# Hash attention: the 32-column products of two pairs of heads gathered in one block of every odd pair

## The chip, the cores and the metric

The kernel runs on one core of a Trainium2 chip. The metric is the device time of one execution in microseconds (us), the median of several runs. A core has five engines with an instruction queue each: TensorE (PE in the profile; its weight loads are shown apart as PEld), VectorE (DVE), ScalarE (ACT), GpSimd (POOL) and SyncE (SP). Each works through its queue in order and waits on semaphores for the others. PE writes PSUM, which DVE and ACT read. DMA queues move data between the core's SBUF and the chip's memory; in this kernel SP issues most of them, POOL and ACT some.

## The reference

Attention with a hash mask, and then a layer with squared relu, all in float32:

```
B, H, S, D = 4, 8, 768, 64           # 6 hash bits, d_model 512, d_ff 2048
q_bits, k_bits = (q @ proj > 0), (k @ proj > 0)
mask   = bucket(q_bits)[:, :, :, None] == bucket(k_bits)[:, :, None, :]
scores = where(mask, q @ k^T / sqrt(D), -1e9)
attn   = softmax(scores);  x = attn @ v        # heads side by side: (3072, 512)
h = x @ w_in;  r = max(h, 0);  out = (r * r) @ w_out
```

A query attends only to keys whose six hash bits are all the same as its own.

## The kernel before, in words

The 32 heads are worked in 16 pairs (`pr` 0 to 15); a pair's two heads lie in the two halves of the 128 partitions. A loop over the pairs is the first stage; the second stage, the squared-relu layer in two levels of Strassen's method, follows and is not touched by the change, except that its tile of three x sums (`t_x`) has its memory allocated early.

The order of the instructions on every engine is written out by hand, inside a manual schedule. Each pair has six key tiles (`kt`), and each key tile two score products (`score`: four matmuls of the hash bits, four of the features, L438), each followed by one exponential on ACT (`weight`, L444) that writes half of a slot of a ring of four key tiles (`e`). Between the score products lie `attend` calls (L492): products of v with the weights, four small matmuls each, two per key tile. A score takes its PSUM buffer from a pool of two (`turn`); so a score waits for the exponential of the score before the last one. The hash products take a buffer of the same pool.

The pairs overlap. While pair `pr` begins, `attend` of key tiles 4 and 5 of pair `pr-1` (`old`) is still going on. After `attend(old, 5, 1)` the old pair is finished in this order: `keep_x` copies its result out of PSUM (ACT, L523); PE runs a block of products that use 32 of the array's columns instead of 64: `sum_up(old, 0)` (half of the softmax totals, L541), `hash_bits(pr + 1)` (the next pair's hash products, L368), `sum_up(old, 1)`; `signs` turns the hash products into signs (ACT, L387); `invert` transposes the totals and takes the reciprocal (DVE, L554, L558, L562); `spread` copies the reciprocals to the other rows (ACT, four small copies, L572); `normalize` transposes them back and scales x (DVE, L578, L584), and SP stores x to memory (`x_all`).

DVE also has, for every pair: `features` (transposes the loaded q and k, L352), `add_up` for key tiles 1 to 5 (adds the weights up to the totals, L475 and L480; a slot of the ring is free for new exponentials only when it has been added and attended to), and the preparation of the weights w_in and w_out, which arrive as 64-bit floats: `part_power` (L150), `part_top` (L176, L180), `round_weight` (L194, L197), and `sum_in` (L600, L617), 16 calls in all, dealt out to the pairs from 4 on. ACT works on the same weights: four `place_power` steps a pair (L166, L168), the last of which comes before `part_top`'s second instruction (L180), which rewrites the same tile. ACT's `weigh` (L393) scales the signs and POOL then places them as bits with eight small DMAs (`place_bits`, L404), for the next pair.

The queue of SP holds, in the order of the program, the loads of q and k (`load_pair`, eight DMAs of 128-byte pieces), of v (`load_values`), of the weights (`load_weight`), and the stores.

What the change touches: the pools and tiles `feat`, `total`, `x_raw`, `signed` and `t_x`; `features` (L349), `weigh` (L391), `sum_up` (L529), `invert` (L551), `normalize` (L574), the sharing out of `sums` (L630) and the body of the pair loop (from L685 on).

Of the kernel before, what the change touches and what calls it, by code (L numbers as in the profile page):

```python
# [8 lines left out]
FP32 = mybir.dt.float32  # L9
# [25 lines left out]
def kernel(  # L35
# [51 lines left out]
    w_out_49 = p_d.tile([7, P, 7, NQ, P], FP32, name="w_out_49")  # L87

    first = ExitStack()
    p_x = first.enter_context(tc.tile_pool(name="p_x", bufs=2))  # L90
# [17 lines left out]
    def spare(name):  # L108

        return ps_t.tile([P, 2, 512], FP32, name=name, tag="spare")  # L110
# [137 lines left out]
    signed = const.tile([P, 2, HS], BF16, name="signed")  # L248
    all_bits = [const.tile([P, 2, S], BF16, name=f"bits{i}") for i in range(2)]

    def constants():
# [20 lines left out]
            nc.vector.memset(e[:, :, :, HS:HS + 1], TINY)  # L272


    nat, feat, bits = {}, {}, {}

    def load_first():

        both = p_qk.tile([P, 2, 2, SB, D], FP32, name="qk_nat")
        for w, src in enumerate((q, k)):  # L280
            for h, queue in enumerate((nc.sync, nc.scalar)):
                queue.dma_start(
                    out=both[:, w, h].rearrange("p t d -> p (t d)"),
                    in_=src[0, h].rearrange("(p t) d -> p (t d)", t=SB),
                )
        nat[0, "qk"] = both
        feat[0] = p_f.tile([P, 2, S], FP32, name="feat")
# [96 lines left out]
    def signs(pr):  # L384


        nc.scalar.activation(  # L387
            out=signed, in_=hashed[pr, 0][:, :, 0:HS], func=ACTF.Sign, scale=HUGE, bias=lifts
        )

    def weigh():  # L391

        nc.scalar.activation(out=signed, in_=signed, func=ACTF.Copy, scale=gains)  # L393

    PARTS = (1, 0), (0, 0), (0, 1), (1, 1)

    def place_bits(pr, parts=PARTS):

        t = all_bits[pr % 2]
        for w, c in parts:  # L400
            bits[pr, w] = t[:, w]
            at = (2 * w + c) * NR_B
            for h in range(2):
                nc.gpsimd.dma_start(  # L404
                    out=t[h * D:h * D + NBITS + 1, w, c * HS:(c + 1) * HS],
                    in_=signed[at:at + NBITS + 1, h],
                )

    def first_keys(c, banks):
# [60 lines left out]
    def add_up(pr, kt):  # L470

        e = key_of(pr, kt)[:, :, :, 0:HS]
        if kt == 1:
            totals[pr] = p_n.tile([P, 2, 2, HS], FP32, name="total")
            nc.vector.scalar_tensor_tensor(  # L475
                out=totals[pr], in0=key_of(pr, 0)[:, :, :, 0:HS], scalar=SB * TINY,
                in1=e, op0=ALU.add, op1=ALU.add,
            )
        else:
            nc.vector.tensor_tensor(out=totals[pr], in0=totals[pr], in1=e, op=ALU.add)  # L480
# [38 lines left out]

    def keep_x(pr):  # L520

        raws_x[pr] = p_n.tile([P, 2, HS + 1], FP32, name="x_raw")
        nc.scalar.copy(out=raws_x[pr], in_=outs.pop(pr)[:, :, 0:HS + 1])  # L523

    NB = HS // 32
    QS = HS // 2
    onces = {}

    def sum_up(pr, s, whole=False):  # L529


        if s == 0:
            spares[pr] = spare("tot")
        halves = [(slice(0, P), s)] if whole else [
            (slice(r * HK, (r + 1) * HK), (r + s) % 2) for r in range(2)
        ]
        for rows, c2 in halves:
            for c in range(2):
                for h in range(2):
                    g = 2 * h + c  # L540
                    done = nc.tensor.matmul(  # L541
                        out=spares[pr][g * 32:(g + 1) * 32, c2, 0:QS], lhsT=ones[rows],
                        rhs=totals[pr][rows, h, c, c2 * QS:(c2 + 1) * QS],
                        start=whole or s == 0, stop=whole or s == 1, skip_group_check=True,
                    )
                    if s and (pr, "tot") in lasts:
                        part(lasts.pop((pr, "tot")), done)
        if not whole and s == 0:
            lasts[pr, "tot"] = done

    def invert(pr):  # L551

        flip = p_n.tile([P, HS], FP32, name="flip")
        nc.vector.transpose(  # L554
            out=flip.rearrange("p (c f) -> p c f", c=2), in_=spares.pop(pr)[:, :, 0:QS]
        )
# [17 lines left out]
    def normalize(pr):  # L574
# [7 lines left out]
        x_t = p_x.tile([P, S], FP32, name="x_t")  # L582
        raw = raws_x.pop(pr)
        nc.vector.scalar_tensor_tensor(  # L584
            out=x_t.rearrange("p (c f) -> p c f", c=2), in0=raw[:, :, 0:HS],
            scalar=raw[:, 0, HS:HS + 1], in1=over.rearrange("p (c f) -> p c f", c=2),
            op0=ALU.add, op1=ALU.mult,
        )
        nc.sync.dma_start(out=x_all[:, j, b * S:(b + 1) * S], in_=x_t)

    PLACE = 0, 5, 6, 1, 2, 3, 4

# [40 lines left out]
    xs = {}  # L633

    def load_x(i, fs=slice(0, NFT)):

        if i not in xs:
            x = p_c.tile([P, NFT, NCH], FP32, name="x")
            xs[i] = x, [p_c.tile([P, 2, NCH // 2], FP32, name=f"t_x{n}") for n in range(3)]
        nc.gpsimd.dma_start(out=xs[i][0][:, fs], in_=x_all[:, fs, i * NCH:(i + 1) * NCH])  # L640

    w_unit = {}
# [21 lines left out]
    with tc.manual_schedule():  # L664
# [18 lines left out]


        for pr in range(NP):  # L685
            more, old = pr + 1 < NP, pr - 1

            def beside(kt, s):
                if pr > 0:
                    attend(old, kt, s)  # L690

            if pr + 2 < NP:
                load_pair(pr + 2)
            if more and pr > 0:
                features(pr + 1)
            if pr == 0:
                first_score()
                first_keys(1, spare("hash"))
            else:
# [38 lines left out]
            if more:  # L738
                score(pr, 2, 0)
            if pr > 0:  # L740
                spread(old)
                attend(pr, 0, 0)
            else:
                attend(pr, 1, 0)
            score(pr, 2, 1)
            if pr > 0:
                attend(pr, 1, 0)
                if more:
                    weigh()
                else:  # L750
                    place_power(pr, 0, 0)
            else:
                hash_bits(1, turn("hash"))
                signs(1)
                weigh()
            score(pr, 3, 0)
            if pr > 0:
                place_power(pr, 0, int(not more))
# [44 lines left out]
        attend(pr, 2, 0)  # L803
        attend_whole(pr, SB - 2)
        add_up(pr, SB - 1)
        for s in range(2):
            sum_up(pr, s, True)
        invert(pr)
        for n in (1, 2, 3):
            sum_x(0, n)  # L810
# [876 lines left out]
```

## Time and profile before

| what | value |
|---|---|
| median of 3 runs | 856.3 us (855.09, 856.30, 856.32) |
| profiled execution, its own time | 855.04 us |
| its span in the trace | 853.2 us |
| busy in the span: PE, DVE, ACT, POOL | 847.0, 749.3, 402.4, 167.4 us |
| granted TensorE clock | 1.00 |
| period of a pair in the middle of the first stage | 19.03 us |
| DVE busy in the pair from 108.43 us on (one sum) | 18.41 us of 19.03 |
| first stage ends, second stage's first matmul | 315.43 us |

The profile lists busy time by engine, groups of instructions by source line, and the chain of work that ended last. The trace can also be asked for the instructions of an engine in order of time, merged where neighbours are alike: start, duration, engine, line, operation, output and inputs, number, and in brackets the idle time before it and what ended it. Busy time counts overlapping instructions once; DVE and ACT instructions that follow each other without a wait overlap by some 0.1 us, so that the distance from start to start is what one of them costs.

### The profile page before, as it was taken

The numbers are of one execution on the slowest core, as the hardware profiler recorded it, in microseconds if no ns is written. First come the engines' busy times: TensorE is split into PE (matmuls) and PEld (weight loads), VectorE is DVE, ScalarE is ACT, GpSimd is POOL, SyncE is SP. The second block draws the span as 40 slices with busy tenths as digits, with TensorE's granted clock in tenths as the row PEclk, the third lists the DMA queues.
The fourth block names the chain that finished last, engine by engine and source line by source line (L and its number), as shares of the span: only waits on it lengthen the run. The fifth ranks groups of instructions, "written<-read, shape, count | busy, mean of one in ns | idle before, by whom it ended". The sixth has DMA issues, their size and how long they took to land.

```text
span 853.2 us, 17058 instructions
## 1 busy us (share of the span) xinstructions
PE 847.0 (99%) x6625; PEld 526.5 (62%) x6625; DVE 749.3 (88%) x1025; ACT 402.4 (47%) x752; POOL 167.4 (20%) x282
## 2 busy tenths in 40 slices
PE   8999999999999999999999999999999999999998
PEld 4544444444444444444788866667888765668886
DVE  5999999999999988988899968888988788889777
ACT  6877777888877752222211145554111355541111
POOL 2311111123221101543122121111000311200003
PEclk9999999999999999999999999999999999999999
DMA  9776988979998526999976985437647865335467
GB/s 213 137 152 143 183 181 203 209 158 258 242 227 217 170 69 225 342 313 297 340 250 220 275 214 189 160 111 283 192 155 189 205 219 171 128 118 161 140 172 147
DMA packets 232052, 170.12 MB, mean 199 GB/s; under 512 B 164712, under 2 KB 189104, under 8 KB 231968
## 3 DMA queue, kind: packets, MB, share of 16 engines
q1 hardware_dynamic: 192272, 87.78, 41.3%
q0 software_dynamic: 16512, 42.45, 15.9%
q10 hardware_dynamic: 23184, 38.78, 14.6%
q8 instruction: 53, 0.87, 0.4%
q14 instruction: 31, 0.25, 0.1%
HBM read 127.14 MB, written 41.16 MB: 197 GB/s over the span
## 4 chain that ended last, share of the span: by engine, by line
PE 97%; DVE 1%; DMA 1%; issue 0%; ACT 0%; SPq 0%; ACTq 0%; DVEq 0%
PE acc L844 39%; PE st L438 18%; PE xo L492 15%; PE acc L1108 13%; PE acc L1061 9%; PE tot L541 2%; PE hash L368 1%; DMA out_dram<-h 1%; DMA qk_nat<-in_q_dram 0%; PE tp L324 0%; DVE h L1224 0%; DVE o L1210 0%; DVE tmp L1210 0%; DVE bits L418 0%; DVE sum L1210 0%
## 5 line engine op out<-in xcount | busy, mean ns | idle before, releaser
L444 ACT ACTIVATE e<-st 128x768 f32<-128x768 f32 x192 | 155.4, 810 | 57.8 <-PE st L438 54.7
L438 PE MATMUL st<-feat 64*64 64x384 f32 x1536 | 156.9, 483 | 0.1
L492 PE MATMUL xo<-e,v_nat 64*64 64x385 f32 (+1 forms) x1520 | 156.7, 483 | 0.0
L844 PE MATMUL acc<-b,leaf 128*128 128x256 f32 x600 | 133.0, 379 | 0.0
L844 PEld LDWEIGHTS acc<-b,leaf 128*128 128x128 f32 x600 | 113.9, 190 | 16.0 <-issue 0.5
L480 DVE TENSOR_TENSOR total<-total,e 128x1536 f32<-128x1536 f32 x64 | 111.8, 1746 | 4.3 <-ACT e L444 2.8
L404 POOL DMA_DIRECT2D bits<-signed x120 | 61.9, 520 | 216.8 <-ACT signed L393 199.9
L492 PEld LDWEIGHTS xo<-e,v_nat 64*64 64x64 f32 (+1 forms) x1520 | 55.5, 133 | 68.2 <-issue 60.2
L1108 PE MATMUL acc<-t_x,w_unit 128*128 128x512 f32 x192 | 90.9, 595 | 0.0
L438 PEld LDWEIGHTS st<-feat 64*64 64x64 f32 x1536 | 55.4, 133 | 38.9 <-issue 34.9
L844 PE MATMUL acc<-t,leaf 128*128 128x256 f32 x336 | 76.0, 379 | 0.0
L844 PEld LDWEIGHTS acc<-t,leaf 128*128 128x128 f32 x336 | 63.8, 190 | 8.8 <-issue 0.2
L921 DVE SCALAR_TENSOR_TENSOR b<-h 128x512 f32<-128x512 f32 x96 | 65.7, 691 | 3.0
L438 PE MATMUL st<-bits 64*64 64x384 bf16 x768 | 64.7, 325 | 0.3 <-DVE bits L422 0.2
L844 PE MATMUL acc<-x,w_unit 128*128 128x512 f32 x128 | 56.5, 593 | 0.0
L851 ACT COPY two<-acc 128x256 f32<-128x256 f32 (+1 forms) x29 | 12.5, 431 | 87.5 <-PE acc L844 65.9
L844 PE MATMUL acc<-b_t,leaf 128*128 128x256 f32 x240 | 53.8, 379 | 0.0
L1108 PEld LDWEIGHTS acc<-t_x,w_unit 128*128 128x128 f32 x192 | 35.8, 190 | 26.7 <-issue 23.0
L1229 POOL DMA_DIRECT2D out_dram<-h x24 | 15.5, 655 | 181.9 <-DVE h L1224 181.9
L844 PEld LDWEIGHTS acc<-b_t,leaf 128*128 128x128 f32 x240 | 45.6, 190 | 6.2
L851 ACT COPY one<-acc 128x256 f32<-128x256 f32 (+1 forms) x29 | 12.5, 431 | 78.2 <-PE acc L844 58.8
L438 PEld LDWEIGHTS <-bits 64*64 64x64 bf16 x768 | 23.2, 107 | 38.0 <-issue 37.9
(180 smaller groups left out, 1289.0 us busy)
## 6 DMA issues: line engine op xcount, KB each, us to landing
leaf<-w_out ACTq DMA_DIRECT2D x142, 256.0 KB, 3.1
raw<-in_moe_w_in_dram SPq DMA_DIRECT2D x8, 1024.0 KB, 6.7
raw<-in_moe_w_out_dram SPq DMA_DIRECT2D x8, 1024.0 KB, 7.9
w_unit<-w_in SPq DMA_DIRECT2D x16, 512.0 KB, 4.1
w_unit<-w_in SPq DMA_DIRECT2D x8, 896.0 KB, 9.0
w_out<-sums POOLq DMA_DIRECT2D x16, 448.0 KB, 8.0
v_nat<-in_v_dram SPq DMA_DIRECT2D x16, 384.0 KB, 5.2
x_all<-x_t SPq DMA_DIRECT2D x16, 384.0 KB, 3.3
```

What stands on the lines that cost most here:

```text
L404: nc.gpsimd.dma_start(out=t[h * D:h * D + NBITS + 1, w, c * HS:(c + 1) * HS], in_=signed[at:at + NBITS + 1, h],)
L438: nc.tensor.matmul(out=st[k * HK:(k + 1) * HK, h, 0:HS], lhsT=src[1][rows, key], rhs=src[0][rows, cut], start=first, stop=not first, skip_ ...
L444: nc.scalar.activation(out=key_of(pr, kt)[:, :, i, 0:HS], in_=st[:, :, 0:HS], func=ACTF.Exp, scale=scale)
L480: nc.vector.tensor_tensor(out=totals[pr], in0=totals[pr], in1=e, op=ALU.add)
L492: return nc.tensor.matmul(out=outs[pr][h * D:(h + 1) * D, c, 0:HS + 1], lhsT=nat[pr, "v_nat"][rows, h, kt * D:(kt + 1) * D], rhs=key_of(pr ...
L541: done = nc.tensor.matmul(out=spares[pr][g * 32:(g + 1) * 32, c2, 0:QS], lhsT=ones[rows], rhs=totals[pr][rows, h, c, c2 * QS:(c2 + 1) * QS ...
L844: nc.tensor.matmul(out=acc[to], lhsT=a(i), rhs=b(i), start=first and i == 0, stop=last and i == n - 1, skip_group_check=True,)
L851: nc.scalar.copy(out=t, in_=acc[of])
L921: nc.vector.scalar_tensor_tensor(out=out, in0=h, scalar=0.0, in1=h, op0=ALU.max, op1=ALU.mult)
L1061: nc.tensor.matmul(out=out, lhsT=w(a), rhs=b, start=start, stop=stop, skip_group_check=True)
L1108: nc.tensor.matmul(out=to, lhsT=w[:, PLACE[a], f], rhs=bt[b](f), start=first and f == 0, stop=last and f == NFT // 2 - 1, skip_group_check ...
L1229: queue.dma_start(out=out[at, m0 + a * 32:m0 + (a + 1) * 32].rearrange("(c i) j -> i c j", i=32), in_=ot[a * 32:(a + 1) * 32].rearrange("i ...
```

## The change

In every odd pair, PE runs one block with the totals of the two pairs before (`pr - 2` and `pr - 1`) and the hash products of the two pairs after (`pr + 1` and `pr + 2`); even pairs have no such block. The last pair has the totals of two pairs in the block and no hash products, and its own totals at the end as before.

For this, three feature buffers are used in turn instead of two, and two tiles of totals instead of one; the third feature buffer and the second totals tile lie in the memory of the three x sums of the second stage, which is now one tile and allocated at the start. `signed` and `x_raw` get a second buffer; x is scaled in place in `x_raw`, and the separate tile `x_t` is gone. `features` and `load_pair` run one pair further ahead: `features(2)` and `features(3)` both in pair 1, and the load of pair 3 in pair 0, ahead of the load of v for pair 1. `invert`, `spread` and `normalize` work on pair `pr - 2`: `invert` behind `part_power` in odd pairs and ahead of `round_weight` in even ones, `spread` behind the second score of key tile 2. The last pair does this for pairs 13 and 14. In even pairs, `attend(pr, 0, 0)` moves behind the second score of key tile 2. The calls of `sum_in` are two in odd and one in even pairs from 4 on, so that pair 15 has none.

```diff
-    p_f = first.enter_context(tc.tile_pool(name="p_f", bufs=2))
+    p_f = first.enter_context(tc.tile_pool(name="p_f", bufs=1))
...
+    def new_x(i):
+        x = p_c.tile([P, NFT, NCH], FP32, name="x")
+        t = p_c.tile([P, 3, 2, NCH // 2], FP32, name="t_x")
+        xs[i] = x, [t[:, n] for n in range(3)]
+        return t.rearrange("p n f c -> p (n f c)")
+
+    early = new_x(0)
+    in_turn = [p_f.tile([P, 2, S], FP32, name=f"feat{n}") for n in range(2)]
+    in_turn.append(early[:, 0:2 * S].rearrange("p (w s) -> p w s", w=2))
+    to_add = [
+        p_n.tile([P, 2, 2, HS], FP32, name="total"),
+        early[:, 2 * S:4 * S].rearrange("p (h c s) -> p h c s", h=2, c=2),
+    ]
...
-        feat[pr] = p_f.tile([P, 2, S], FP32, name="feat")
+        feat[pr] = in_turn[pr % 3]
...
-            totals[pr] = p_n.tile([P, 2, 2, HS], FP32, name="total")
+            totals[pr] = to_add[(pr + 1) % 2]
...
+    def sums_and_hashes(prs, nexts):
+        if not nexts:
+            return sum_whole(prs)
+        new_totals(prs)
+        sum_up(prs[0], 0)
+        for n, nxt in enumerate(nexts):
+            hash_bits(nxt, turn("hash"))
+            signs(nxt)
+            if n < len(prs):
+                sum_up(prs[n], 1)
+            if n + 1 < len(prs):
+                sum_up(prs[n + 1], 0)
...
-        n = 16 if pr == NP - 1 else 1 + (pr % 3 == 0)
+        n = 1 + pr % 2
...
-            if pr + 2 < NP:
-                load_pair(pr + 2)
-            if more and pr > 0:
-                features(pr + 1)
+            if pr == 0:
+                load_pair(2)
+            elif pr + 3 < NP:
+                load_pair(pr + 3)
+            if 0 < pr < NP - 2:
+                features(pr + (2 if pr > 1 else 1))
...
                 add_up(old, SB - 1)
+                if not odd:
+                    invert(pr - 2)
                 if pr == 1:
+                    features(3)
                     part_top(0)
                 round_weight(old)
...
                 features(1)
+                load_pair(3)
             else:
                 keep_x(old)
-                sum_up(old, 0)
-                if more:
-                    hash_bits(pr + 1, turn("hash"))
-                    signs(pr + 1)
-                else:
-                    score(pr, 2, 0)
-                sum_up(old, 1)
-                invert(old)
+                if odd:
+                    sums_and_hashes(
+                        range(max(pr - 2, 0), pr), [n for n in (pr + 1, pr + 2) if n < NP]
+                    )
             add_up(pr, 1)
...
             part_power(pr)
+            if odd and pr > 1:
+                invert(pr - 2)
...
-            if pr > 0:
-                spread(old)
+            score(pr, 2, 0)
+            if odd:
                 attend(pr, 0, 0)
...
             score(pr, 2, 1)
             if pr > 0:
+                if pr > 1:
+                    spread(pr - 2)
+                if not odd:
+                    attend(pr, 0, 0)
                 attend(pr, 1, 0)
...
             add_up(pr, 2)
+            if pr > 1:
+                normalize(pr - 2)
             if pr > 0:
-                normalize(old)
...
+            if not more:
+                invert(old)
             add_up(pr, 3)
...
             attend(pr, 2, 1)
+            if not more:
+                spread(old)
+                normalize(old)
             score(pr, 4, 1)
```

More of the change, by code (lines that the diff above doesn't have):

```diff
@@ L247 @@
     ring = [const.tile([P, 2, 2, HS + 1], FP32, name=f"e{i}") for i in range(NRING)]
-    signed = const.tile([P, 2, HS], BF16, name="signed")
+    signed = [const.tile([P, 2, HS], BF16, name=f"signed{i}") for i in range(2)]
     all_bits = [const.tile([P, 2, S], BF16, name=f"bits{i}") for i in range(2)]
@@ L286, in load_first @@
         nat[0, "qk"] = both
-        feat[0] = p_f.tile([P, 2, S], FP32, name="feat")
+        feat[0] = in_turn[0]
         for h, queue in enumerate((nc.sync, nc.scalar)):
@@ L387, in signs, with weigh @@
         nc.scalar.activation(
-            out=signed, in_=hashed[pr, 0][:, :, 0:HS], func=ACTF.Sign, scale=HUGE, bias=lifts
+            out=signed[pr % 2], in_=hashed[pr, 0][:, :, 0:HS], func=ACTF.Sign, scale=HUGE, bias=lifts
         )
-    def weigh():
-        nc.scalar.activation(out=signed, in_=signed, func=ACTF.Copy, scale=gains)
+    def weigh(pr):
+        t = signed[pr % 2]
+        nc.scalar.activation(out=t, in_=t, func=ACTF.Copy, scale=gains)
     PARTS = (1, 0), (0, 0), (0, 1), (1, 1)
@@ L527, with new_totals @@
     onces = {}
+    tots = {}
+    def new_totals(prs):
+        to = spare("tot")
+        for n, pr in enumerate(prs):
+            tots[pr] = to[:, :, n * QS:(n + 1) * QS], n
+            spares[pr] = tots[pr][0]
     def sum_up(pr, s, whole=False):
-        if s == 0:
-            spares[pr] = spare("tot")
+        to, n = tots[pr]
         halves = [(slice(0, P), s)] if whole else [
-            (slice(r * HK, (r + 1) * HK), (r + s) % 2) for r in range(2)
+            (slice(r * HK, (r + 1) * HK), (r + s + n) % 2) for r in range(2)
         ]
@@ L545, in sum_up, with sum_whole @@
                     )
[L546 to L549, printed above, removed]
+                    if s and not whole and "tot" in lasts:
+                        part(lasts.pop("tot"), done)
+        if not whole:
+            lasts["tot"] = done
+    def sum_whole(prs):
+        new_totals(prs)
+        for pr in prs:
+            for s in range(2):
+                sum_up(pr, s, True)
+    def sums_and_hashes(prs, nexts):
+        if not nexts:
+            return sum_whole(prs)
+        new_totals(prs)
+        sum_up(prs[0], 0)
[6 more added lines that the diff above has]
+                sum_up(prs[n + 1], 0)
     def invert(pr):
@@ L554, in invert @@
         nc.vector.transpose(
[L555 removed]
+            out=flip.rearrange("p (c f) -> p c f", c=2), in_=spares.pop(pr)
         )
@@ L685 @@
         for pr in range(NP):
-            more, old = pr + 1 < NP, pr - 1
+            more, old, odd = pr + 1 < NP, pr - 1, pr % 2
             def beside(kt, s):
@@ L805 @@
         add_up(pr, SB - 1)
-        for s in range(2):
-            sum_up(pr, s, True)
+        sum_whole((pr,))
         invert(pr)
```

32 lines of the change are left out of this document (14 added, 18 removed).

## The prediction

> **What bounds the kernel now.** I read the busy times first, then the chain that ended last, then PE, ACT and DVE in order of time over one pair, and last the two ends of the first stage. Busy times and chain:
>
> ```profile
> PE 847.0 (99%) x6625; PEld 526.5 (62%) x6625; DVE 749.3 (88%) x1025; ACT 402.4 (47%) x752; POOL 167.4 (20%) x282
> PE 97%; DVE 1%; DMA 1%; issue 0%; ACT 0%; SPq 0%; ACTq 0%; DVEq 0%
> ```
>
> PE bounds nearly all of it, so the kernel gets faster only where PE does less, and slower wherever PE starts to wait. PE around the block that is regrouped:
>
> ```profile
> 49.95 0.81 PE L438 MATMUL st<-feat 64*64 64x384 f32 x8
> 50.60 0.82 PE L492 MATMUL xo<-e,v_nat 64*64 64x385 f32 x8
> 51.34 0.56 PE L541 MATMUL tot<-total,ones 64*32 64x192 f32 x16
> 51.69 0.85 PE L368 MATMUL hash<-feat,projs 64*32 64x384 f32 x16
> 52.34 0.53 PE L541 MATMUL tot<-total,ones 64*32 64x192 f32 x16
> 52.80 0.36 PE L438 MATMUL st<-bits 64*64 64x384 bf16 x4
> 52.99 0.81 PE L438 MATMUL st<-feat 64*64 64x384 f32 x8
> ```
>
> Read the distances between starts: a group of feats costs 0.65 (49.95 to 50.60), a step of score and attend 1.455, the pair 19.03. Twelve steps are 17.46, so the block costs 1.57. Its products stream 0.32 + 0.65 + 0.32 = 1.29 (the attends before it would end at 51.25), which leaves 0.28, mostly at the two changes between 64 and 32 columns: 0.09 going in, 0.14 to 0.17 coming out.
>
> DVE and ACT stand close behind. A stretch of each, in the pair whose totals come at 184.55:
>
> ```profile
> 186.43 0.58 DVE L554 STREAM_TRANSPOSE flip<-tot 128x384 f32<-128x384 f32 x1
> 187.39 1.75 DVE L475 SCALAR_TENSOR_TENSOR total<-e,e 128x1536 f32<-128x1536 f32 x1
> 189.06 0.69 DVE L150 TENSOR_SCALAR power<-raw 128x1024 uint32<-128x1024 uint32 x1
> 194.94 0.69 DVE L176 TENSOR_SCALAR top<-raw 128x1024 uint32<-128x1024 uint32 x1
> 195.72 1.23 DVE L180 SCALAR_TENSOR_TENSOR power<-raw,power 128x1024 uint32<-128x1024 uint32 x1
> 204.25 0.68 DVE L617 TENSOR_TENSOR s_in<-in 128x512 f32<-128x512 f32 x1
> 205.22 0.58 DVE L554 STREAM_TRANSPOSE flip<-tot 128x384 f32<-128x384 f32 x1 [0.28 <-PE tot L541]
> ```
>
> ```profile
> 187.09 0.81 ACT L444 ACTIVATE e<-st 128x768 f32<-128x768 f32 x1 [0.32 <-PE st L438]
> 187.93 0.83 ACT L572 COPY rec<-once 32x12 f32<-32x12 f32 x4
> 188.78 0.81 ACT L444 ACTIVATE e<-st 128x768 f32<-128x768 f32 x1
> 189.62 0.94 ACT L393 ACTIVATE signed<-signed,gains 128x768 bf16<-128x768 bf16 x1
> 190.46 0.79 ACT L444 ACTIVATE e<-st 128x768 f32<-128x768 f32 x1
> 195.07 0.62 ACT L168 ACTIVATE power<-small 128x512 uint32<-128x512 uint8 x1
> ```
>
> From 186.43 to 204.25 DVE does a pair's work without the sums, without a gap, in 17.82; only L180 waits there, for the L168 that ends at 195.69 (L176 takes 0.78 to the next start, the like L150 0.60), so 17.64 are its own. A sum adds 0.60. With one sum DVE fills 18.24 of 19.03, with two 18.84. And it is tied to ACT: the reciprocals (L562) release `spread` (L572), behind which in ACT's queue stand `weigh` (L393), the exponentials and `place_power` (L166, L168), and the last of these releases L180.
>
> **The change part by part.**
>
> *Fewer blocks.* Before there are 16 (one in each of pairs 1 to 14; in pair 15 a score divides the totals, which makes two: 298.73 to 300.64 holds 0.55 beyond products). After there are 8. The products stay the same. 8 x 0.28 = **-2.2 us**. PE's two pairs then cost 2 x 17.46 + 4 x 0.32 + 2 x 0.65 + 0.28 = 37.8 instead of 38.06.
>
> *The loop through DVE and ACT (pairs 5, 7, 9, 11, 13).* Two pairs now have three sums: DVE needs 2 x 17.64 + 3 x 0.60 = 37.1 of 37.8, and that alone would fit. But in odd pairs `invert` stands behind two sums, `add_up` 1 and `part_power`, and `spread` behind the second score of key tile 2. Follow one L180 in an odd pair to the next odd pair's. DVE runs everything in between up to the reciprocals, that is 37.1 without what comes later in the odd pair (`add_up` 2, `normalize`, `add_up` 3, L176: 1.67 + 1.95 + 1.67 + 0.60 = 5.9) and with 0.1 until ACT sees the result: 31.3. Then ACT: `spread` 0.85, and from `weigh`'s start to L168's end 195.69 - 189.62 = 6.07, some 0.1 less where the exponentials needn't wait for PE: 6.85. The loop takes 38.2, and PE would like 37.8. The missing 0.4 falls on PE: with `spread` and `weigh` behind the exponential that PE releases 1.46 after the one before, key tile 3's first exponential ends some 0.1 before the first score of key tile 4 needs its PSUM buffer even when nothing is late (before: 58.06 against 58.64). Every later `spread` is a PE wait. Adding 0.05 for restarting PE, 5 x 0.45 = **+2.2**. Bounds: 0 if DVE's instructions overlap a little more in the new order, 3 if the scaled x, written with gaps into `x_raw` (L584's 1.02 is for a dense tile), takes 0.1 longer. Pairs 1 and 3 have no sums, their loop is 36.4, and nothing waits.
>
> *The start.* Pair 1's block needs `features(3)`, whose load is moved ahead of v's. SP issues in before:
>
> ```profile
> 19.73 3.05 SPq L299 DMA_DIRECT2D qk_nat<-in_k_dram  x4
> 22.83 0.53 SPq L312 DMA_DIRECT2D v_nat<-in_v_dram  x1
> 23.45 3.88 SPq L299 DMA_DIRECT2D qk_nat<-in_q_dram  x4
> 27.38 3.90 SPq L299 DMA_DIRECT2D qk_nat<-in_k_dram  x4
> ```
>
> The DMA engines are full there (share 1.0 to 1.4 from 24 to 30 us), so pair 3's eight DMAs, issued from 22.83 on, still take 7 to 8 us: the last lands at 32 to 34 (27.38 + 3.9 + a landing of 2.6, less 0.6 to 2 for v out of the way). DVE gets there at 29.4 and stands; `features` takes 1.77; the second hash products would start at 33.65 (32.31 + 0.35 + 0.65 + 0.34) and start at 34 to 36. I take **+1.0** (0 to 2.4). v for pair 1 is issued some 7.8 later, at 30.6, and with its 5.1 lands at 35.7, just when `attend(1, 0, 0)` comes after that wait. DVE, 3 us late in pair 1, has no `normalize` there to do and no PE wait hangs on it; w_in's next piece is asked for 7 later and has the pair to land.
>
> *The last pair.* Here two pairs are inverted and normalized, while the sums and `features` are gone. Count from the block's start. DVE: `add_up` 2 waits for the exponential at 4.9; then 1.67, `normalize(13)` 1.95, `invert(14)` 0.96, `add_up` 3 1.67, `normalize(14)` 1.95, `add_up` 4 and 5 1.67 + 1.75: ends at 16.5. Before, `add_up` 5 ended at 313.14 - 298.73 = 14.4, and the totals followed at once:
>
> ```profile
> 313.19 0.86 PE L541 MATMUL tot<-total,ones 128*32 128x192 f32 x16
> ```
>
> PE by itself could start them 0.3 earlier (310.23 + four groups of 0.65), and in after 0.4 later (totals of two pairs in the block, one change fewer): 14.2 and 14.5. The wait grows from 0.3 to 2.0: **+1.7** (1.2 to 2.0). Behind it the stages keep their distances.
>
> *What costs nothing.* Two `signs` in one block: the second (0.9) lies between the second hash products and an exponential that PE releases later. The `attend` moved in even pairs covers `keep_x` (0.8), which would otherwise be waited for, as no block lies before it: without that, 0.35 a pair. The stores of x in two pieces a row: 384 KB, 3.3 us to landing, no reader near. POOL's queue: `place_bits` (4.14) follows `weigh`; in odd pairs it ends some 0.3 before the `attend` that needs a POOL step behind it, less than ACT's delay, so it moves with that. SP: stores and loads keep their places in the middle of a pair.
>
> [...] DVE's additions of 1.75 are followed by the next start after 1.67 (187.39 to 189.06): they overlap. [...]
>
> *Sum:* -2.2 + 2.2 + 1.0 + 1.7 = **+2.7**, and 0.1 for the second exponential behind two `signs` in pair 1: +2.8. The profiled execution took 855.04 (span 853.2 and 1.8 around it), which gives 857.8. The three runs are 855.09, 856.30 and 856.32, so the profiled one is 1.3 below the median; their mean is 855.9, and I put 2.8 on that: **858.7 us**.
>
> **The rivals.** About 0.2% (1.7 us) is what a measurement of this kernel can tell from no change.
>
> *The forecast (chance 0.48):* loop, start and last pair all cost; 857.4 to 860.
>
> *The loop doesn't bind (0.25).* DVE delivers the odd pair's reciprocals before ACT wants them. For it: only 0.4 of 38 is missing. Against: ACT has no room even then. -2.2 + 0 to 1 + 1.0 + 1.7: 856.4 to 857.4, within 0.2%.
>
> *The gain arrives whole (0.10), the other side.* One mechanism: DVE has slack. It decides where the reciprocals come less than 3.2 after the block's end and, by the same speed, the last additions less than 14.5 after the block's start; then -2.2 and a start that costs nothing: 853.7. Against it: DVE's gapless 17.82.
>
> *The start is worse (0.12).* Pair 3's load shares the DMA engines with more than I see, and lands at 36 or later; hash products, v and the bits of pair 2 all wait: +2 more, 860.7. With a gap over 3.4 us, the Trainium skill (TensorE: Matmul & The Clock Gate, Part 1) would have PE's clock halved for about as long, an estimate of 1.7 us more; no wait here that long is in the trace, and every row shows a granted clock of 1.00.
>
> *The change doesn't do what it says (0.05).* If the 0.28 sits at totals and hash products and not at the change of columns, a double block pays it twice: -2.2 becomes 0, 860.9. Against: 51.34 to 52.34 is 1.00, of which products are 0.97.
>
> **How the numbers follow.** Faster holds the third case: 0.10. Same holds the second: 0.25. Slower holds the others: 0.65. The range leaves out half of the third case and the far end of the fourth: 855.0 to 861.5.
>
> **What would show it.** The odd pair's block near 2.86 and no such block in even pairs; PE waits of 0.4 to 0.6 in odd pairs from 5 on, at a score (L453 in after), put down to ACT; ACT's `rec` copies waiting for DVE; DVE standing at `features(3)` near 30 us; the last pair's totals some 2 us after PE is free. I am wrong if two pairs take 37.8 in the middle of the stage, or if DVE's scaling of x changes from 1.02.

## The result, and the profile after

The changed kernel takes 861.27 us in the median (858.95 to 863.09), the kernel before 856.31: ratio 1.0059, interval 1.0042 to 1.0076, slower by 0.6 per cent. The forecast was 858.7, slower, with a range up to 861.5. The sign and the two terms of the middle came out nearly as worked. Some 2.6 us were not foreseen; the traces show two places that the prediction had put at nothing, and a start that differs from run to run. The profiled execution took 860.77 with a span of 859.2, 5.7 and 6.0 more than the one of before.

Busy times and the chain that ended last, after:

```profile
PE 849.3 (99%) x6593; PEld 554.8 (65%) x6593; DVE 748.3 (87%) x1025; ACT 401.0 (47%) x752; POOL 169.0 (20%) x282
PE 84%; DVE 8%; ACT 3%; issue 2%; DMA 1%; POOL 0%; DVEq 0%; SPq 0%; ACTq 0%; POOLq 0%
```

DVE had 1 per cent of the chain and has 8: PE now runs beside work that it must wait for. The double block of pair 9, PE in order of time (start, length, then the operation):

```profile
185.67 0.56 PE L564 MATMUL tot<-total,ones 64*32 64x192 f32 x16
186.02 0.85 PE L382 MATMUL hash<-feat,projs 64*32 64x384 f32 x16
186.67 0.53 PE L564 MATMUL tot<-total,ones 64*32 64x192 f32 x16
186.99 0.53 PE L564 MATMUL tot<-t_x,ones 64*32 64x192 f32 x16
187.32 0.85 PE L382 MATMUL hash<-t_x,projs 64*32 64x384 f32 x16
187.96 0.53 PE L564 MATMUL tot<-t_x,ones 64*32 64x192 f32 x16
188.42 0.36 PE L453 MATMUL st<-bits 64*64 64x384 bf16 x4
```

From 185.67 to 188.42 it takes 2.75, against 1.46 for one block before (51.34 to 52.80): the second totals follow the first within 0.32, and the 0.46 from the last totals to the first score is paid once. What it does to the engines behind it, in the same pair, from DVE's, ACT's and PE's rows:

```profile
191.94 0.18 DVE L608 COPY rec<-once 128x24 f32<-128x24 f32 x1
199.03 1.22 DVE L179 SCALAR_TENSOR_TENSOR power<-raw,power 128x1024 uint32<-128x1024 uint32 x1 [0.67 <-ACT power L167]
```

```profile
192.15 0.83 ACT L618 COPY rec<-once 32x12 f32<-32x12 f32 x4 [0.32 <-DVE rec L608]
193.01 0.94 ACT L408 ACTIVATE signed<-signed,gains 128x768 bf16<-128x768 bf16 x1
193.85 0.79 ACT L459 ACTIVATE e<-st 128x768 f32<-128x768 f32 x1
```

```profile
194.69 0.36 PE L453 MATMUL st<-bits 64*64 64x384 bf16 x4 [0.26 <-ACT e L459]
```

This is the loop of the prediction, link by link: ACT waits 0.32 for the reciprocals, PE a quarter of a microsecond for the exponential behind `weigh`, DVE 0.67 for the power. L179 of the odd pairs stands at 84.09, 122.44, 160.80 and 199.03, so 38.35, 38.36 and 38.23 apart; 38.2 was forecast for the loop alone.

The end of the first stage, PE and then DVE:

```profile
312.49 2.91 PE L507 MATMUL xo<-e,v_nat 64*64 64x385 f32 x24
317.43 1.20 PE L564 MATMUL tot<-total,ones 128*32 128x192 f32 x16 [2.03 <-DVE total L495]
318.56 2.81 PE L507 MATMUL xo<-e,v_nat 128*64 128x385 f32 x8
321.30 3.70 PE L899 MATMUL acc<-x,w_unit 128*128 128x512 f32 x8
```

```profile
311.82 0.97 DVE L624 STREAM_TRANSPOSE recs<-rec 128x768 f32<-128x768 f32 x1
312.82 1.02 DVE L630 SCALAR_TENSOR_TENSOR x_raw<-x_raw,recs 128x768 f32<-128x768 f32 x1
313.76 3.61 DVE L495 TENSOR_TENSOR total<-total,e 128x1536 f32<-128x1536 f32 x2
```

The wait of 2.0 us is there as forecast. Not forecast: behind it the same totals take 1.20 in place of 0.86 and the attends 2.81 in place of 1.52. The stretches of 1 us show why (length, then busy time and number of instructions of PE, PEld, DVE, ACT and POOL, then the granted clock, the DMA share and GB/s):

```profile
317.00:318.00 1.00, 0.57 (x12) 0.47 (x16) 0.37 (x1) 0.00 (x0) 0.00 (x0) 0.90 0.00 0
318.00:319.00 1.00, 1.00 (x10) 0.30 (x4) 0.33 (x1) 0.00 (x0) 0.00 (x0) 0.50 0.00 0
320.00:321.00 1.00, 1.00 (x6) 0.14 (x2) 0.97 (x2) 0.61 (x4) 0.00 (x0) 0.50 0.00 0
```

By stretches of 0.5 us the clock was at half from 317.8 to 321.2, 3.4 us. Last totals to second stage take 3.87 instead of 2.24.

The table has the same landmarks in the kernel before and in every kernel with the double block. The distances are between the starts of the blocks of pairs 1, 3, 5 and so on, "tail" is from pair 15's block to the last totals and from these to the first matmul of the second stage, "first" is the length of PE's first 36 transposes:

```
kernel          first  1-3   3-5   5-7   7-9   9-11  11-13 13-15  tail         median (runs)
before           2.35  38.06 38.06 38.06 38.06 38.06 38.06 38.06  14.46  2.24  856.31 (6)
changed          3.58  37.30 37.93 38.35 38.36 38.85 38.19 37.98  16.74  3.87  861.27 (6)
e11_again        2.27  38.33 37.93 38.36 38.35 40.33 37.92 38.27  16.73  2.24  860.49 (1)
e1_late_norm     2.27  37.30 37.93 38.36 38.36 39.81 37.93 38.26  15.57  2.23  858.84 (7)
e3_fill          2.47  37.30 37.93 38.33 38.35 42.20 37.92 38.22  16.73  2.24  861.32 (5)
e5_swap_tail     2.88  37.30 37.92 38.37 38.35 40.49 37.93 38.22  16.83  0.79  858.05 (8)
e2_early_invert  2.91  37.29 37.93 37.93 37.94 38.53 37.93 38.00  16.74  3.36  859.46 (4)
e4_both          2.38  37.30 37.93 37.93 37.93 38.68 37.93 38.16  15.59  2.23  857.53 (12)
e6_late_features 2.48  37.52 37.92 38.41 38.58 38.51 39.14 37.93  16.74  2.23  860.40 (4)
e9_raw_later     3.71  37.29 37.93 38.35 38.36 38.59 40.89 37.92  16.74  2.89  862.73 (4)
e7_all           2.29  37.29 37.78 37.77 37.78 38.34 37.77 37.78  15.93  0.79  855.11 (9)
e10_all_raw      3.30  37.30 37.77 37.78 37.77 37.78 40.63 37.77  15.94  0.79  857.59 (12)
```

(Where the tail ends in 0.79, the 1.45 of the last attends has moved to the column before it. 1-3 is 0.65 short in every row but the first because pair 1's block has the totals of one pair alone; they come back in pair 15's block.)

Of the profiled 6.0 us, by this table: 1.4 in the first 8 us, 0.5 between the blocks of pairs 1 and 15, 2.3 up to the last totals, 1.6 by the halved clock, 0.1 behind it.

### The profile page after: what moved, and what is told of

Its sections match the earlier page's. It is cut to its first block, busy times and chain, and to the rows that moved or that the text cites. A ratio compares the mean times of both kernels' runs of the same rounds, so it can differ in the third digit from the quotient of the medians.

```text
span 859.2 us, 17029 instructions
## 1 busy us (share of the span) xinstructions
PE 849.3 (99%) x6593; PEld 554.8 (65%) x6593; DVE 748.3 (87%) x1025; ACT 401.0 (47%) x752; POOL 169.0 (20%) x282
## 4 chain that ended last, share of the span: by engine, by line
PE 84%; DVE 8%; ACT 3%; issue 2%; DMA 1%; POOL 0%; DVEq 0%; SPq 0%; ACTq 0%; POOLq 0%
PE acc L899 39%; PE acc L1163 13%; PE st L453 12%; PE xo L507 9%; PE acc L1116 8%; DVE t_x L495 2%; DVE total L495 1%; ACT e L459 1%; PE tot L564 1%; PE hash L382 1%; DMA out_dram<-h 1%; DMA bits<-signed 1%; DVE total L490 1%; DVE top L193 1%; DVE x_raw L630 0%
## 5 line engine op out<-in xcount | busy, mean ns | idle before, releaser
L507 PE MATMUL xo<-e,v_nat 64*64 64x385 f32 (+1 forms) x1520 | 162.1, 485 | 0.0
L453 PE MATMUL st<-feat 64*64 64x384 f32 x1056 | 111.7, 483 | 0.1
L507 PEld LDWEIGHTS xo<-e,v_nat 64*64 64x64 f32 (+1 forms) x1520 | 67.1, 133 | 57.8 <-issue 48.5
L453 PE MATMUL st<-bits 64*64 64x384 bf16 x768 | 70.4, 324 | 1.6 <-ACT e L459 1.0
L495 DVE TENSOR_TENSOR total<-total,e 128x1536 f32<-128x1536 f32 x32 | 55.9, 1747 | 4.3 <-ACT e L459 3.9
L495 DVE TENSOR_TENSOR t_x<-t_x,e 128x1536 f32<-128x1536 f32 x32 | 55.8, 1745 | 2.9 <-ACT e L459 2.8
L453 PEld LDWEIGHTS st<-feat 64*64 64x64 f32 x1056 | 43.6, 133 | 20.5 <-issue 18.1
L453 PEld LDWEIGHTS <-bits 64*64 64x64 bf16 x768 | 29.8, 106 | 37.4 <-issue 34.6
L453 PE MATMUL st<-t_x 64*64 64x384 f32 x480 | 50.6, 482 | 0.0
```

What stands on the lines that cost most here:

```text
L453: nc.tensor.matmul(out=st[k * HK:(k + 1) * HK, h, 0:HS], lhsT=src[1][rows, key], rhs=src[0][rows, cut], start=first, stop=not first, skip_ ...
L507: return nc.tensor.matmul(out=outs[pr][h * D:(h + 1) * D, c, 0:HS + 1], lhsT=nat[pr, "v_nat"][rows, h, kt * D:(kt + 1) * D], rhs=key_of(pr ...
```

## The experiments

### The loop: invert earlier (e2_early_invert), and split the blocks (e8_split_block)

```diff
+            if odd and pr > 1:
+                invert(pr - 2)
             add_up(pr, 1)
...
             part_power(pr)
-            if odd and pr > 1:
-                invert(pr - 2)
```

> The changed kernel, but in the odd pairs VectorE inverts the totals of the pair before last ahead of the add of 1.75 us and the shift of 0.69 us, so the reciprocal is there about 2.3 us earlier. Theory that a loop of VectorE and ScalarE (reciprocal, spread, weighing, exponentials, powers, the or of 1.22 us) sets the two pairs: TensorE's work of 37.8 us is the limit again, the distance of two pairs falls from 38.35 in the mean (37.98 to 38.85) to 37.8, the wait of VectorE for the power (0.67 us, seven times) and of TensorE's scores for the exponentials go, in all 2 to 2.8 us less than the changed kernel, about 858.5 to 859.3. Rival, the double block itself or its clock makes the two pairs long: the distances stay at 38.2 to 38.5, no change, 861.

859.46, ratio to before 1.0038 (1.0023 to 1.0052), 1.8 us less than the changed kernel, a little under the 2 to 2.8 expected. Pairs 5-7 and 7-9 fall from 38.35 to 37.93, so the loop was the limit there; that they stop at 37.93 and not at 37.8 was not expected. PE's two pairs in the middle, 108.07 to 146.00 (same columns as above):

```profile
108.07:146.00 37.93, 37.93 (x580) 20.80 (x576) 37.07 (x36) 29.66 (x47) 8.43 (x16) 1.00 0.89 189
```

PE counts as busy throughout, but from the attend at 116.02 to the next score is 0.13 more than its products need, at the place where ACT has `spread` and `weigh` (0.83 and 0.94) behind one another. e7_all below takes `spread` away from there, moves `features` as well, and reaches 37.78 with no such gap in the odd pairs' rows.

e8 puts one more change of columns into each pair of the kernel before:

```diff
                     signs(pr + 1)
-                else:
-                    score(pr, 2, 0)
+                score(pr, 2, 0)
                 sum_up(old, 1)
...
-            if more:
+            if pr == 0:
                 score(pr, 2, 0)
```

> The kernel before, with the second half of each pair's totals behind the first score of key tile 2 in pairs 1 to 14, as pair 15 has it: the same products, one more change from 64 to 32 columns and back in each pair. If such a change costs 0.28 us for in and out together: a pair takes 19.26 to 19.31 in place of 19.03, 14 of them 3.2 to 3.9 us more, about 859.5 to 860. If the 0.28 belongs to the block and not to the changes: 19.03, 856.3. If the later reciprocals make VectorE and ScalarE late, waits of TensorE for the exponentials show, and the pair grows by more than 0.3.

860.84 (one run); the pair takes 19.35, in 13 of 14 pairs, which is 0.32 more (0.23 to 0.28 was expected), with no wait of PE above 0.2 us in the first stage behind the start. The price sits at the change between 64 and 32 columns; the rival "it sits at the totals themselves" is out.

### The tail: e1_late_norm, e5_swap_tail, e3_fill

```diff
             if not more:
                 spread(old)
-                normalize(old)
...
         normalize(pr)
         sum_x(0, 4)
+        normalize(old)
```

(with a second buffer for the two small tiles of reciprocals.)

> The changed kernel, but in the last pair VectorE scales x of pair 14 (the transpose of 0.97 us and the scale of 1.02 us) only behind the last sum of the second stage's x, and no longer ahead of the last two adds. Theory that the tail is VectorE's queue and then the clock: the last two adds start about 1.9 us earlier, TensorE waits under 0.4 us for the total in place of 2.03, its granted clock stays at 1.00 from 316 to 322 us, and from the start of the last totals to the first matmul of the second stage it takes about 2.3 us as in the kernel before (3.87 in the changed one); in all 3 to 3.5 us less than the changed kernel, about 857.5 to 858.2. Rival, the clock falls there for another reason: only 1.7 us less, about 859.5. Rival, the end of the first stage is covered by the second (weights or x not there yet): no change, 861.

858.84 (ratio 1.0035, 1.0022 to 1.0049). The wait is 0.86 and not under 0.4, since the last two adds now wait 0.69 for an exponential. The clock stays at 1.00. Pair 15's block to the second stage: 17.80 against 20.61, so 2.8 less, as expected of queue and clock, with 0.5 of it missed. Of the 2.8, 1.2 are totals that come earlier (15.57 against 16.74); the other 1.6 are the clock, which stayed up in some executions with the wait too (e11 and e6 below).

```diff
         add_up(pr, SB - 1)
+        attend_whole(pr, SB - 1)
         sum_whole((pr,))
...
+        keep_x(pr)
         spread(pr)
-        attend_whole(pr, SB - 1)
-        keep_x(pr)
```

> The changed kernel, but in the last pair the eight value products of key tile 5 (1.52 us) stand ahead of the last totals and not behind them, so that TensorE has work while VectorE does the last two adds; the totals start when they did. If the tail costs what it costs because the wait of 2.03 us stands alone and lets the clock fall: the wait splits off to about 0.5 us, the granted clock stays at 1.00, and from the start of pair 15's block to the first matmul of the second stage it takes about 17.6 us (20.61 in the changed kernel, 16.70 in the one before), 3.0 us less, about 858.3. If the clock falls after a shorter wait too, 19 to 20 us and 859.5 to 860.5. If the second stage waits for the last x rather than for TensorE: no change, 861.

858.05 (ratio 1.0024, 1.0010 to 1.0037). Block to second stage 17.62; the wait is 0.82, the clock 1.00. Work that needs no DVE, put into the wait, is worth 3.0 us against the first profile, and 1.35 against the changed kernel's second profile (e11, 16.73 + 2.24), which had the wait without the fall of the clock.

e3 puts nine matmuls that nobody reads ahead of the last totals:

```diff
         add_up(pr, SB - 1)
+        fill = turn("fill")
+        for _ in range(9):
+            nc.tensor.matmul(
+                out=fill[:, 0], lhsT=busy, start=True, stop=True,
+                rhs=busy.rearrange("p (o n) -> p o n", o=1).to_broadcast([P, 4, P]),
+            )
         sum_whole((pr,))
```

> The changed kernel, with 9 matmuls of 128 x 512 in bf16 on a constant tile (output never read, some 1.9 us in all) on TensorE ahead of the last totals, in the place where it waits 2.03 us. If the wait is what lets the clock fall: the granted clock stays at 1.00 there, the totals start when they did (317.4 us, or 0.1 to 0.3 later), and from them to the second stage it takes 2.3 us in place of 3.87: about 1.3 to 1.6 us less than the changed kernel, 859.7 to 860.0. If the clock falls there for another reason (a limit on power or a slot of time): 861 to 861.5.

861.32 (ratio 1.0060, 1.0039 to 1.0080): no gain in the median, although the tail did what was expected (totals at 16.73, then 2.24, clock 1.00). That the fill kept the clock up is not shown by it: e6 and e11 have the wait without the fill, and 2.23 and 2.24 too. The profiled execution had lost 3.85 elsewhere, between the blocks of pairs 9 and 11, and there too a wait of 2 us was followed by a halved clock:

```profile
218.91 0.46 PE L453 MATMUL st<-bits 64*64 64x384 bf16 x4 [1.99 <-DMA bits<-signed]
221.17 1.74 PE L453 MATMUL st<-t_x 64*64 64x384 f32 x8
```

```profile
218.00:220.00 2.00, 1.09 (x16) 1.00 (x20) 2.00 (x2) 0.00 (x0) 0.56 (x1) 0.97 0.83 176
220.00:222.00 2.00, 2.00 (x19) 1.45 (x15) 2.00 (x2) 0.81 (x1) 0.00 (x0) 0.50 1.01 277
```

Eight products of features take 1.74 there, 0.84 elsewhere. This was the first sight of a loss that the prediction does not have: pair 11's first scores wait for their bits.

### The bits of pair 11: e6_late_features, e9_raw_later

In most rows of the table 9-11 is longer than its neighbours, by 0.5 to 3.9. What SyncE (SPq, its DMA issues) and POOL issue in pair 10, and how long the eight copies of bits take to land (minimum, median, maximum), before:

```profile
204.36 0.35 SPq L211 DMA_DIRECT2D w_out<-out_piece  x1
206.33 1.02 SPq L140 DMA_DIRECT2D raw<-in_moe_w_out_dram  x1
209.88 4.09 POOL L404 DMA_DIRECT2D bits<-signed  x8 [13.17 <-ACT signed L393]
DMA to landing us min/median/max: 3.4/4.0/4.9
```

and in the changed kernel:

```profile
208.64 0.35 SPq L210 DMA_DIRECT2D w_out<-out_piece  x1
210.57 0.74 SPq L139 DMA_DIRECT2D raw<-in_moe_w_out_dram  x1
211.18 4.11 POOL L419 DMA_DIRECT2D bits<-signed  x8 [11.18 <-ACT signed L408]
DMA to landing us min/median/max: 4.5/5.7/6.4
```

The store of the rounded piece (`w_out<-out_piece`) waits for DVE, 0.3 us before and 2.2 in the changed kernel, and SP's queue holds the load of 1 MB (`raw`) behind it. Before, that load goes out 3.55 ahead of the bits; now 0.61, and in e3 0.12, where the copies take 6.5 to 8.4. Two runs test it.

```diff
-            if 0 < pr < NP - 2:
+            if 0 < pr < NP - 2 and odd:
                 features(pr + (2 if pr > 1 else 1))
...
                 round_weight(old)
+                if 0 < pr < NP - 2 and not odd:
+                    features(pr + 2)
```

> The changed kernel, but in even pairs VectorE's transpose of the features (1.77 us) stands behind the rounding of the weight, so the rounded piece is there about 1.8 us earlier, and with it the stores and the load of 1 MB that SyncE issues behind it. If pair 11's first scores wait for their bits because that load, late in the changed kernel, shares the DMA engines with the eight copies of bits: the copies land 3.5 to 5 us after their issue (3.4 to 4.9 before, 4.5 to 6.4 in the changed kernel, up to 8.4 in another run), no score waits for bits, the distance from the block of pair 9 to that of pair 11 falls from 38.85 (38.53 to 42.20 in the others) to the 38.35 of its neighbours: 0.5 us less, about 860.8, and a smaller spread of the runs. If another transfer, or the load of the second stage's x, delays the bits: the wait stays, 861.

860.40 (ratio 1.0046, 1.0031 to 1.0062). The load goes out 2.2 ahead of the bits, no score of pair 11 waits for them, and 9-11 is level with 7-9. But they land after 4.2 to 5.8, not 3.5 to 5, a wait of 0.2 for bits turned up in pair 12, and the distances beside it grew (38.58, 39.14). No clear gain, and half of an answer.

```diff
-                if more:
+                if more and pr != 10:
                     load_weight(pr + 1)
...
                 load_values(pr + 1)
+            if pr == 10:
+                load_weight(pr + 1)
```

> The changed kernel, but in pair 10 alone the load of 1 MB of raw weight (row raw<-in_moe_w_out_dram) stands behind the copies of pair 11's bits and the load of v, not ahead of them. If that load, issued 0.1 to 0.6 us ahead of the bits in the changed kernel and its variants and 3.55 us ahead in the kernel before, is what makes the bits late: they land 3.5 to 5 us after their issue (median 5.7 in the changed kernel, 4.0 before), neither a score nor its weight load waits for bits in pair 11, and pair 9's block to pair 11's takes 38.35 as its neighbours do (38.85 in the changed kernel): 0.5 to 1.5 us less than the changed kernel in the median, about 860. If the other stores of pair 10 (512 KB twice, 256 KB) do as much: landings of 5 us and more, 38.5 to 40.

The copies of pair 11's bits in this run, and PE at the first scores of pairs 12 and 13:

```profile
DMA to landing us min/median/max: 1.5/2.1/3.4
```

```profile
240.66 0.44 PE L453 MATMUL st<-bits 64*64 64x384 bf16 x4 [1.70 <-DMA bits<-signed]
259.09 0.44 PE L453 MATMUL st<-bits 64*64 64x384 bf16 x4 [0.71 <-DMA bits<-signed]
```

The load is the cause: without it ahead of them the bits of pair 11 land in 1.5 to 3.4, and 9-11 loses all but 0.2. How much it delays them is not set by its lead alone: in e7_all below it goes out 2.3 ahead, and the copies still land after 5.7 in the median. The expected gain did not come: the load now stands behind, q and k of pair 13 behind it, so that the next load of 1 MB goes out 1.7 ahead of pair 12's bits (5.3 in the changed kernel), and the bits of pairs 12 and 13 are late instead (11-13 takes 40.89). 862.73, ratio 1.0075 (1.0060 to 1.0090), the slowest of all.

### Putting it together: e4_both, e7_all, e10_all_raw

> Both edits, the late scale of pair 14 and the early inversion. If the two losses are separate and those of the theory: 5 to 6.3 us less than the changed kernel, 855.0 to 856.3, which is between 1.3 us faster and as fast as the kernel before (856.3). If the two share a cause: about 858.

857.53 (ratio 1.0012, 1.0003 to 1.0021), 3.7 less than the changed kernel and not 5 to 6.3. The pairs and the tail did what e1 and e2 did alone; what its profile still lacks is in 9-11 (38.68, with 0.45 of waiting for bits) and in the 0.87 of waiting at the last totals. But the profiled execution took 855.38, as expected and the shortest of the 12; where the median's other 2 us lie, this trace can't show.

e7_all has e1, e2, e5 and e6 in one kernel, and the spread one score earlier in odd pairs:

```diff
             score(pr, 2, 0)
             if odd:
+                if pr > 1:
+                    spread(pr - 2)
                 attend(pr, 0, 0)
...
             score(pr, 2, 1)
             if pr > 0:
-                if pr > 1:
-                    spread(pr - 2)
                 if not odd:
+                    if pr > 1:
+                        spread(pr - 2)
                     attend(pr, 0, 0)
```

> Five edits on the changed kernel: pair 14's scale behind the second stage's sums, the inversion ahead of the add in odd pairs, the spread of the reciprocals one score earlier in odd pairs, the features behind the rounding in even pairs, the value products of key tile 5 ahead of the last totals. If all the losses found are losses of order: two pairs take 37.80 (38.06 before, 37.93 with the early inversion alone), no wait of TensorE above 0.1 us in pairs 3 to 14, the tail from the block of pair 15 to the second stage 17.0 us; together 854.5 to 855.5 in the median, 0.8 to 1.8 us faster than the kernel before. If the spread is not what TensorE waited 0.13 us for: two pairs stay at 37.93, 855.5 to 856.3.

855.11 (853.66 to 856.13), ratio 0.9979, interval 0.9969 to 0.9989: faster than the kernel before by 0.2 per cent, 6.2 less than the changed one. PE's waits from 34 us to the last totals (total, times, longest), and the tail:

```profile
PE st L453 <- ACT e L459: 0.3, 1, 0.3
```

```profile
311.66 1.14 PE L507 MATMUL xo<-e,v_nat 128*64 128x385 f32 x6
312.73 0.86 PE L564 MATMUL tot<-total,ones 128*32 128x192 f32 x16
313.52 3.70 PE L903 MATMUL acc<-x,w_unit 128*128 128x512 f32 x8
```

Two pairs take 37.78, five times, 0.28 less than before: with nothing to wait for, the double block saves just what the prediction took for the change of columns. Block to second stage is 16.72 (16.70 before). 9-11 still has 0.56 too much. In this profile 2.4 us of the gain are lost again behind the first stage: 0.5 of them up to the last matmul, 2.0 behind it (from its start to the end of the span 5.8 us, 3.9 before). What causes that is open.

> The kernel with the five edits of order, and the raw load of pair 10 later as well. If the load makes the bits late: pair 9's block to pair 11's takes 37.78 as its neighbours do (38.34 with the five edits), the weight load of pair 11's first score no longer waits 0.9 us for bits, 0.5 to 0.6 us less than with the five edits: 854.5 in the median, 0.2 per cent faster than the kernel before and more. If not: 855.1.

857.59 (ratio 1.0019, 1.0010 to 1.0028): a miss. 9-11 takes 37.78 as expected, and 11-13 takes 40.63, as in e9. Moving the load only moves the collision.

### The changed kernel once more: e11_again

> The changed kernel as it is, once more, for what differs from run to run. If the slow first transposes (3.58 us; the six other kernels with the same start had 2.27 to 2.91) and the fall of the clock behind the wait of 2.03 us come with the moment and not with the kernel, they may be there or not: first transposes of 2.3 to 3.6, totals to second stage 2.24 or 3.3 to 3.9. The wait of 2.03 itself, the double blocks and two pairs of 38.35 in the middle stay to within 0.1. If both belong to the kernel: 3.58 and 3.87 again.

860.49. The wait of 2.02, the blocks and 38.35 are there again; the slow first transposes and the fall of the clock are not. In their place are 1.5 more in 9-11 (40.33 against 38.85), and a wait at the start, PE and DVE:

```profile
33.40 0.53 PE L564 MATMUL tot<-t_x,ones 64*32 64x192 f32 x16
34.83 0.56 PE L382 MATMUL hash<-feat,projs 64*32 64x384 f32 x8 [0.90 <-DVE feat L366]
```

```profile
32.91 1.78 DVE L366 STREAM_TRANSPOSE feat<-qk_nat 128x1536 f32<-128x1536 f32 x1 [2.91 <-DMA qk_nat<-in_k_dram]
```

That is the forecast cost of `features(3)`, 1.03 in 1-3. It shows in this execution, 0.2 in e6's, and in none of the nine others with this start, where DVE waits (1.13 in the changed kernel's first profile) but the hash products do not.

## Why the prediction was right, and where it was not

*Fewer blocks, -2.2: right.* e7_all has 37.78 in place of 38.06, e8 pays 0.32 for each change added.

*The loop, +2.2: right in mechanism and nearly in size.* 38.35 was measured for 37.8 + 0.45 = 38.25, and e2 removes it. The scaling of x kept its 1.02. In the first profile PE loses 0.55, 0.57 and 0.42 at the place worked out in pairs 5, 7 and 9, and only 0.13 and 0.18 in pairs 11 and 13, behind the wait for bits: 1.85 for five times 0.45. A small term was missing: "Pairs 1 and 3 have no sums, their loop is 36.4, and nothing waits". 3-5 takes 37.93, 0.15 over, for `spread` and `weigh` in one step, as e7_all suggests; 1-3 is 0.17 over in the changed kernel and in e7_all alike: the score behind pair 1's block starts 0.96 behind the second hash products (35.05 to 36.01) and not 0.79. The gain of the change is therefore eaten in the middle, and a little more: pair 1's block to pair 15's is 0.5 more in the profile, or 1.2 with the 0.65 that 1-3 is short. Seven double blocks saved 2.0; of the 3.2 lost, 1.85 are the loop, 0.3 are pairs 1 and 3, and the other 1.0 lie in and around the wait for pair 11's bits.

*The start, +1.0 (0 to 2.4): an event, not a constant.* It cost 0, 0.2 or 1.0. Of the 1.4 that the first profile lost there, 1.2 are the first transposes; e8, which has the start of the kernel before, has 3.28, so the change did not make them slow.

*The last pair, +1.7: right.* DVE's last add was forecast to end 16.5 after the block's start; it was 16.7. The totals came 2.28 later than before, and 0.65 of that is the totals that pair 1's block lacks: 1.6.

*"Behind it the stages keep their distances": wrong.* Behind a wait of 2 us the clock was at half in three of five executions that had the wait in the tail (changed, e2, e9: 3.87, 3.36, 2.89), and not in two (e6, e11: 2.23, 2.24). That is 0.65 to 1.6, or nothing. e1 and e5, with waits under 0.9, kept the clock.

*"SP: stores and loads keep their places in the middle of a pair": wrong, and the larger miss.* The terms for DVE's lateness were followed to ACT and PE and not to SP's queue, where the rounded piece is waited for. In even pairs it comes 3 us later against the bits, and the load of 1 MB behind it lands on the DMA engines together with the copies of pair 11's bits: 9-11 took 0.5 too much in the first profile, 2.0 in e11, 1.5 in e1, 3.9 in e3. I put this at nothing and gave no row for it.

Together: the forecast's +2.8 with the start at 0 to 1 is 1.8 to 2.8; bits of 0.5 to 4 and a clock of 0 to 1.6 can make up the rest of the 5.0 between the medians. How often each comes can't be said from one or two profiles per kernel, and the later loops take up part of a wait (11-13 is 37.92 behind a long 9-11). The median lies above the 857.4 to 860 of the case that I held most likely. That it still lies in the range, 0.2 below its upper end of 861.5, is partly luck: that end was drawn for other cases, a worse start above all, and the loss came from the bits and the clock.

Of the rivals, "the loop doesn't bind" and "the gain arrives whole" fall with 38.35 and e2, "doesn't do what it says" with e7_all and e8. "The start is worse" had the right kind of cause, a load that shares the DMA engines with more than I saw, and the right kind of aftermath, a halved clock, in the wrong places.

## What to carry to other kernels

When a change makes an engine late, follow it into the DMA queues that wait for its results, too: in this kernel a large transfer that started 3 us later landed on small copies that had room before, and that loss differed from run to run. A saving on a full PE is only had when the loops through the other engines are shorter than PE's new period; here five moves of order turned 0.6 per cent slower into 0.2 per cent faster. Work that needs no other engine belongs where PE will have to wait.

## What the runs showed of the hardware

- Behind a wait of 2.0 us on PE the granted clock can fall to half. It did so in four of six places with waits of 1.99 to 2.03 (the tail of the changed kernel, e2 and e9, the bits in e3), each time for 3.4 us, from 0.4 to 1.5 us behind the end of the wait; behind waits of 1.7 and less (e5, e9, e11 at the bits) it never did. The Trainium skill (TensorE: Matmul & The Clock Gate, Part 1) puts the fall after an idle window of some 3.4 us; here 2.0 were enough. The Trainium skill also says there that the window runs free, so that when the clock changes depends on where in it the first matmul falls; that the same wait had the fall in some executions and not in others agrees.
- The first 36 transposes, the same in all kernels, took from 2.27 to 3.71 us, with a granted clock of 1.00 in the rows. The Trainium skill (TensorE: Matmul & The Clock Gate, Part 1) says that the first matmuls vary from run to run with that window; no run here shows that this is the reason. What decides it was not tested.
- The same eight copies of 5 KB landed after 2.1 us in the median when the load of 1 MB was issued behind them (e9; stores of 512 KB and twice 256 KB had gone out up to 2.9 us ahead), and after 7.3 with the load issued 0.12 us ahead of them (e3). In between the lead does not order the times: 5.7 with 0.61 us (changed) and with 2.3 us (e7_all), 4.0 with 3.55 us (before).
